# Narrowing the feed-forward weights in other groups: w_out shifted by one block, a transpose of q in two pieces

## The chip, the cores and the metric

The kernel runs on one core of one Trainium2 chip. A core has five engines that run side by side: TensorE (PE in the profile, with its weight loads as PEld), VectorE (DVE), ScalarE (ACT), GpSimd (POOL) and SyncE (SP), which here issues most of the transfers. The metric is the device time of one execution in microseconds (us), as the median of three runs: 303.51 us before the change (303.37 to 304.15).

## The reference

Two blocks follow one another. The first is a linear attention with a polynomial sketch: q and k are projected by S1 and S2, and the outer product of the two projections is the feature map. Its numerator divided by its denominator is the input x of a gated feed-forward layer.

```python
# batch, heads, seq, head_dim = 4, 4, 1088, 32;  r = 8
def phi(x):
    a = np.einsum('rd,bhsd->bhsr', S1, x)
    b = np.einsum('rd,bhsd->bhsr', S2, x)
    return np.einsum('bhsi,bhsj->bhsij', a, b).reshape(*x.shape[:-1], r * r)
q_p, k_p = (phi(q), phi(k))
kv = np.einsum('bhsf,bhsd->bhfd', k_p, v)
z = np.sum(k_p, axis=2)
num = np.einsum('bhsf,bhfd->bhsd', q_p, kv)
den = np.einsum('bhsf,bhf->bhs', q_p, z)[..., None] + 1e-06
attn = num / den                       # -> x: (4352 tokens, 128)

# w_gate, w_val: (128, 1536);  w_out: (1536, 128)
gate = 1.0 / (1.0 + np.exp(-(x @ w_gate)))
val = x @ w_val
out = gate * val @ w_out
```

S1, S2 and the three weights arrive as 64-bit floats, since they were divided by a 64-bit square root. The kernel sees each as two 32-bit words and has to narrow it to a 32-bit float itself, with integer operations.

## The kernel before

The 1536 hidden columns are 12 blocks (NJ = 12) of 128. The 4352 tokens are taken in chunks of 512 and a rest of 256. One "wave" (`w1`) multiplies a chunk by one block of w_gate and one of w_val; ScalarE takes the sigmoid; `glu` multiplies gate by val on VectorE; `w2` multiplies the product by the block of w_out and adds it to the chunk's output in PSUM. `slot` runs waves and puts the `w2` of a block behind the wave of the next.

```python
def slot(group, waves):
    if group is not None:
        group()
    todo = moe["todo"]
    for _ in range(waves):
        ...
        glu()                      # product of the wave before
        ...                        # lag = 2 (3 at the very end)
        while len(todo) >= lag:
            w2(*todo.pop(0))       # second layer, one block behind
        if more:
            w1()                   # next wave
```

The narrowing of one group of weights is a generator. Its steps use three engines; the caller decides between which other instructions each step is placed. PE, VectorE, ScalarE and GpSimd carry out their instructions in the order of the program.

```python
def narrow(out, bits, eng, bank=None, copies=None):
    cap, tail = tmp(I32, "cap", 6), tmp(I32, "tail", 5)
    eng.tensor_scalar(out=cap.bitcast(F32), in0=hi..., ...)        # GpSimd
    nc.scalar.activation(out=tail, in_=lo, func=ACTF.Copy, ...)    # ScalarE
    yield                                                          # step 0
    head = tmp(I32, "head", 3)
    nc.vector.tensor_scalar(out=head, in0=cap, ...)                # L105
    nc.vector.scalar_tensor_tensor(out=head, in0=cap, ..., in1=head, ...)  # L109
    yield                                                          # step 1
    square = cap.bitcast(F32)
    if bank:
        square = pso.tile([P, 512], F32, tag=bank, name="square")...
    nc.scalar.activation(out=square, in_=cap.bitcast(F32), func=ACTF.Square)
    nc.gpsimd.tensor_tensor(out=head, in0=head, in1=tail, op=ALU.add)      # L118
    yield                                                          # step 2
    nc.vector.scalar_tensor_tensor(out=out, in0=square, ..., in1=head, ...)  # L127
    yield                                                          # step 3
```

`pso` holds one tile per tag in PSUM, and its tags "acc0" and "acc1" are one bank each. The outputs of even chunks accumulate in acc0, those of odd ones in acc1; while one is in use the other is free for squares and for the denominators.

The groups before the change are: gate and val of block 0, gate and val of block 1, w_out of blocks 0 and 1 together (256 elements in a row each), then for j = 2 to 11 gate, val and w_out of block j (384 elements). A wave of chunk 0 carries the steps of the blocks that follow:

```python
def narrow_w(j, step):
    ...
        narrowing[j] = narrow(
            w_sb[:, :, j, :], w_in[n][:, :, jj], nc.gpsimd, "acc1" if j < NJ - 2 else None)

# in w1, after the sigmoid:
if ci == 0:
    if j0 == 1:
        narrow_01(2, 3)
    if 0 < j0 < NJ - 2:
        narrow_w(j0 + 1, 3)
    narrow_w(j0 + 2, 1)
    narrow_w(j0 + 2, 2)
    if j0 < 3:
        narrow_w(j0 + 3, 0)
    if j0 > 1:
        narrow_w(j0 + 4, 0)
```

Chunk 0 is interleaved with the rest of batch 0. Its second half of tokens needs a compact projection of q (`qcomp`, tile cqps), which goes out to DRAM and comes back spread over the partitions (`spread`, tiles qp and bq), a product of the two (`qmult`), and then denominators and numerators (`dn`, tiles dps and nps).

```python
def dn(b, n, mid=None, pool=(ps2, "two")):
    if b == 0:
        bank = (moe["sum"] + 1) % 2 if moe["sum"] >= 0 else 1
        dps = pso.tile([P, TCH], F32, tag=f"acc{bank}", name="dps")
    ...                                  # PE: dps, then nps
    def divide(...):
        ...                              # turn, add 1e-6, first(), reciprocal, transpose, product

slot(None, 1)                            # wave 0
slot(None, 1)                            # wave 1
turn_q(0, 1)                             # transpose of q, 576 wide, VectorE
slot(None, 1)                            # wave 2
slot(q01, 6)                             # cqps and spread, then waves 3 to 8
qmult(0, 1)
load_kq(1)
slot(None, 1)                            # wave 9
slot(lambda: part01(lambda: narrow_w(NJ - 1, 3)), 1)   # dn(0, 1), wave 10
slot(last01, 1)                          # last product of x, wave 11
```

Of the kernel before, what the change touches and what calls it, by code (L numbers as in the profile page):

```python
# [8 lines left out]
F32 = mybir.dt.float32  # L9
I32 = mybir.dt.int32  # L10
# [10 lines left out]
def kernel(  # L21
# [30 lines left out]
    const = ctx.enter_context(tc.tile_pool(name="const", bufs=1))  # L52
    ld = ctx.enter_context(tc.tile_pool(name="ld", bufs=1))
    sbA = ctx.enter_context(tc.tile_pool(name="sbA", bufs=2))
    raw = ctx.enter_context(tc.tile_pool(name="raw", bufs=NJ // 2))
    sbN = ctx.enter_context(tc.tile_pool(name="sbN", bufs=1))
    sbG = ctx.enter_context(tc.tile_pool(name="sbG", bufs=6))

# [24 lines left out]
    def narrow(out, bits, eng, bank=None, copies=None):  # L83

        p, n, m = bits.shape[:3]
        lo, hi = bits[:, :, :, 0].bitcast(U32), bits[:, :, :, 1]

        def tmp(dt, tag, bufs):
            return sbN.tile([P, 3, P], dt, tag=tag, name=tag, bufs=bufs)[:p, :n, :m]

        cap, tail = tmp(I32, "cap", 6), tmp(I32, "tail", 5)
        eng.tensor_scalar(  # L97
            out=cap.bitcast(F32), in0=hi.bitcast(F32), scalar1=122880.0, scalar2=-122880.0,
            op0=ALU.min, op1=ALU.max,
        )  # L100
        nc.scalar.activation(out=tail, in_=lo, func=ACTF.Copy, scale=2.0**-29)  # L101
        yield

        head = tmp(I32, "head", 3)
        nc.vector.tensor_scalar(  # L105
            out=head, in0=cap, scalar1=3, scalar2=0x3FFFFFF8,
            op0=ALU.logical_shift_left, op1=ALU.bitwise_and,
        )
        nc.vector.scalar_tensor_tensor(  # L109
            out=head, in0=cap, scalar=-0x40000000, in1=head, op0=ALU.bitwise_and, op1=ALU.bitwise_or  # L110
        )
        yield
        square = cap.bitcast(F32)
        if bank:
            square = pso.tile([P, 512], F32, tag=bank, name="square")[:, : n * m]
            square = square.rearrange("p (n m) -> p n m", n=n)
        nc.scalar.activation(out=square, in_=cap.bitcast(F32), func=ACTF.Square)  # L117
        nc.gpsimd.tensor_tensor(out=head, in0=head, in1=tail, op=ALU.add)  # L118
        yield

        head = head.bitcast(F32)
        if copies:
            square, head = (
                bass.AP(tensor=x.tensor, offset=x.offset, ap=[list(x.ap[0]), [0, copies], [1, m]])
                for x in (square, head)
            )
        nc.vector.scalar_tensor_tensor(  # L127
            out=out, in0=square, scalar=1.265625 * 2.0**-30, in1=head, op0=ALU.is_ge, op1=MUL
        )
        yield  # L130
# [11 lines left out]
                nc.sync.dma_start(out=rows, in_=s_)  # L142


    w_sb = const.tile([P, 3, NJ, P], F32, tag="w_sb", name="w_sb")
    w_in = {}

    def load_w_in(j0, j1):
        cs = slice(j0 * P, j1 * P)
        n, jj = divmod(j0, 2)  # L150
        if wide and jj == 0:
            w_in[n] = raw.tile([P, 3, 2, P, 2], I32, tag="w_in", name="w_in")
        for i, src in enumerate((moe_w_gate, moe_w_val)):
            if wide:
                nc.sync.dma_start(
                    out=w_in[n][:, i, jj : jj + j1 - j0].rearrange("p j m w -> p (j m w)"),
                    in_=src[:, cs].bitcast(I32),
                )
            else:
                nc.sync.dma_start(  # L160
                    out=w_sb[:, i, j0:j1].rearrange("p j m -> p (j m)"), in_=src[:, cs]
                )

    def load_w_out(n):
        j0, j1 = 2 * n, 2 * n + 2
        cs = slice(j0 * P, j1 * P)
        src = moe_w_out[cs, :].bitcast(I32) if wide else moe_w_out[cs, :]
        nc.sync.dma_start(
            out=w_in[n][:, 2].rearrange("p j m w -> p j (m w)") if wide else w_sb[:, 2, j0:j1],
            in_=src.rearrange("(j p) m -> p j m", p=P),  # L170
        )

    narrowing = {}

    def narrow_w(j, step):
        if not 0 <= j < NJ:
            return
        n, jj = divmod(j, 2)
        if wide:
            if step == 0:  # L180
                narrowing[j] = narrow(
                    w_sb[:, :, j, :], w_in[n][:, :, jj], nc.gpsimd, "acc1" if j < NJ - 2 else None
                )
            next(narrowing[j])


    def narrow_01(part, step):
        if wide:
            if step == 0:
                i = (slice(0, 2), part) if part < 2 else (2, slice(0, 2))  # L190
                narrowing["01", part] = narrow(
                    w_sb[:, i[0], i[1]],
                    w_in[0][:, i[0], i[1]],
                    nc.gpsimd,
                    "acc0" if part else "acc1",
                )
            next(narrowing["01", part])


    def load_rows(src, b, t, parts=((0, T, nc.sync),)):  # L200
# [42 lines left out]
    load_w_in(0, 1)  # L243
    v_t[0] = load_v(0)
    load_w_in(1, 2)
    load_w_out(0)
    load_rows(q, 0, q_t[0], ((T0, T, nc.sync),))
    for n in range(1, NJ // 2):
        load_w_in(2 * n, 2 * n + 2)
        load_w_out(n)  # L250


    def warm(*cols):
# [53 lines left out]
    def w2(ci, j0, jn, g):  # L307
# [4 lines left out]
        for jj in range(jn):  # L312
            j = j0 + jj
            nc.tensor.matmul(  # L314
                out=moe["acc"][:, :tw],
                lhsT=w_sb[:, 2, j, :],
                rhs=g[:, jj, :tw],
                start=(j == 0),
                stop=(j == NJ - 1),
            )  # L320
        if j0 + jn == NJ:
# [6 lines left out]
            while c < t0 + tw:  # L328
# [13 lines left out]
                    )  # L342
                c += n * 32

    def w1():

        ci = moe["ci"]
        t0, tw = tok_chk[ci]
        jn = TCH // tw
        j0 = moe["w"] * jn  # L350
        wv = psm.tile([P, 2, TCH], F32, tag="wave", name="wave")

        tp = tw // 2 if ci == 0 and j0 == 0 else tw
        for o in range(0, tw, tp):
            for which in range(2):
                for jj in range(jn):
                    nc.tensor.matmul(  # L357
                        out=wv[:, which, jj * tw + o : jj * tw + o + tp],
                        lhsT=w_sb[:, which, j0 + jj, :],
                        rhs=xT[:, t0 + o : t0 + o + tp],  # L360
                        start=True,
                        stop=True,
                    )
        sg = sbG.tile([P, TCH], F32, tag="sg", name="sg", bufs=3)
        nc.scalar.activation(out=sg, in_=wv[:, 0], func=ACTF.Sigmoid)  # L365
        if ci == 0:
            if j0 == 1:
                narrow_01(2, 3)
            if 0 < j0 < NJ - 2:
                narrow_w(j0 + 1, 3)  # L370
            narrow_w(j0 + 2, 1)
            narrow_w(j0 + 2, 2)
            if j0 < 3:
                narrow_w(j0 + 3, 0)
            if j0 > 1:
                narrow_w(j0 + 4, 0)


        def glu():
            g = sbG.tile([P, TCH], F32, tag="g", name="g")  # L380
            nc.vector.tensor_tensor(out=g, in0=wv[:, 1], in1=sg, op=MUL)  # L381
            moe["todo"].append((ci, j0, jn, g.rearrange("p (j t) -> p j t", j=jn)))

        moe["gate"] = glu
        moe["w"] += 1
        if j0 + jn == NJ:
            moe["ci"] += 1
            moe["w"] = 0
# [38 lines left out]
            in_=k_t[b][:, t0:t1].rearrange("p t d -> p (t d)"),  # L427
        )

    def turn_q(b, n):  # L430
        if b >= B:
            return
        if n == 0:
            qT_of[b] = sbA.tile([P, TP, 2, 32], F32, tag="qT", name="qT", bufs=1)
        t0, tn = q_chk[n]
        nc.vector.transpose(  # L436
            out=qT_of[b][:, t0 : t0 + tn].rearrange("p t c s -> p (t c s)"),
            in_=q_t[b][:, 2 * t0 : 2 * (t0 + tn)].rearrange("p t d -> p (t d)"),
# [214 lines left out]
    def qmult(b, n):  # L653
        q0 = half(QP[b], n)
        nc.vector.tensor_tensor(out=q0, in0=q0, in1=half(BQ[b], n), op=MUL)  # L655

    def kv0(j_list):
        if 0 not in KVZ:
# [34 lines left out]
            )  # L693

    def kvd(b):
        KVD[b] = sbA.tile([P, 2, 2, F], F32, tag="kvd", name="kvd")
        k0 = KVZ[b][:, : 2 * F]
        n = 2 if b > 0 else 1
        nc.scalar.copy(
# [211 lines left out]

    if wide:
        steps = narrow(s4, s_in, nc.vector, copies=4)
        for _ in range(3):
            next(steps)
    turn_k(0, 0, KBASE[2] + 1)
    if wide:
# [54 lines left out]
    for part in range(2):  # L972
        narrow_01(part, 0)
    spread_z()
    warm(512)
    for pi in range(2):
# [6 lines left out]
    def rest(turn, rc, dT):  # L983
# [8 lines left out]
        narrow_01(0, 1)  # L992
        narrow_01(0, 2)
        ndt(0)

    divide = dn(0, 0, rest)
    warm(256)

    def head1():
        narrow_01(1, 1)  # L1000
        narrow_01(0, 3)
        narrow_01(1, 2)
        narrow_01(2, 0)
        narrow_w(2, 0)

    divide((0, 4), (4, 8), between=head1)
    narrow_01(1, 3)
    narrow_01(2, 1)
    narrow_01(2, 2)

    slot(None, 1)
    cq = {}
# [33 lines left out]
        kv(b, ZS[b])  # L1046
        kvd(b)

    slot(None, 1)
    turn_q(0, 1)  # L1050
    slot(None, 1)
    slot(q01, 6)
    qmult(0, 1)
    load_kq(1)
    slot(None, 1)
    slot(lambda: part01(lambda: narrow_w(NJ - 1, 3)), 1)
    slot(last01, 1)
    v_t[1] = load_v(1)
    for b in range(1, B):
# [60 lines left out]
```

## Time and profile before

| | before |
|---|---|
| median of three runs | 303.51 us |
| span in the profile | 301.7 us |
| PE busy | 295.3 us (98%) |
| VectorE busy | 154.7 us (51%) |
| ScalarE busy | 80.7 us (27%) |
| GpSimd busy | 33.0 us (11%) |
| first wave starts | 15.18 us |
| last narrowing ends (L127) | 45.0 us |
| wave 0 of chunk 1 starts | 48.35 us |

The table is an average over stages. Up to 15 us the attention of the first tokens is computed; from 15 to 48 us chunk 0 runs beside the narrowing and the second part of batch 0, and VectorE is busy for 7.96 of 8.40 us between 15.18 and 23.58 and 13.56 of 17.39 between 23.58 and 40.97; afterwards the matmuls follow one another, and the attention of batches 1 to 3 lies between them. In the profile a matmul of 512 columns in 32-bit floats is two records, so a wave counts four.

### The profile page before, as it was taken

What the parts mean: (1) busy time and instruction counts of PE and PEld (TensorE: products, weight loads), DVE (VectorE), ACT (ScalarE), POOL (GpSimd) and SP (SyncE); (2) the same over time, 40 slices, a digit from 0 to 9 for tenths busy, and PEclk for the clock granted to TensorE, in tenths of its full rate; (3) what the DMA queues carried; (4) which work ended last, traced back from release to release, by engine and by line L of the source; (5) the groups of instructions that cost most, each with busy time, mean ns of one, the idle gap of its engine ahead of it and who ended that gap; (6) DMA issues with size and microseconds to landing.
All of it is one profiled execution on the core that took longest, in us unless ns stands there. A gap on an engine that the chain in (4) does not pass through costs nothing.

```text
span 301.7 us, 3642 instructions
## 1 busy us (share of the span) xinstructions
PE 295.3 (98%) x1363; PEld 137.3 (46%) x1363; DVE 154.7 (51%) x268; ACT 80.7 (27%) x150; POOL 33.0 (11%) x62
## 2 busy tenths in 40 slices
PE   8899999999999999999999999999999999999994
PEld 3444434453444444434444445344444444444683
DVE  6997789764635545383365444932232223222331
ACT  3556533222122222212232222122222222222220
POOL 1465550410000400000004000000000000000000
PEclk9999999999999999999999999999999999999999
DMA  7993440897101591350016900200020000100011
GB/s 226 358 337 89 103 144 6 201 223 192 42 15 19 136 225 35 77 187 0 0 27 168 218 17 2 36 2 0 0 32 3 0 0 12 25 0 0 9 28 18
DMA packets 30546, 24.24 MB, mean 80 GB/s; under 512 B 20480, under 2 KB 25728, under 8 KB 30528
## 3 DMA queue, kind: packets, MB, share of 16 engines
q1 hardware_dynamic: 27024, 16.15, 20.5%
q0 software_dynamic: 2592, 7.08, 10.5%
q10 hardware_dynamic: 912, 0.77, 1.0%
q8 instruction: 11, 0.18, 0.2%
q14 instruction: 7, 0.06, 0.1%
HBM read 20.73 MB, written 3.26 MB: 80 GB/s over the span
## 4 chain that ended last, share of the span: by engine, by line
PE 86%; DVE 5%; DMA 3%; issue 2%; POOL 2%; ACT 1%; SPq 0%; DVEq 0%; POOLq 0%; ACTq 0%
PE wave L357 52%; PE moeout L314 27%; DMA bq<-dq 2%; PE nps L861 2%; POOL head L118 1%; PE kvz L677 1%; DVE head L109 1%; DVE w_sb L127 1%; DVE qp L655 1%; DMA s_in<-in_S_dram 1%; PE kps L456 1%; DVE head L105 1%; PE cqps L602 0%; PE deni L811 0%; PE dps L841 0%
## 5 line engine op out<-in xcount | busy, mean ns | idle before, releaser
L357 PE MATMUL wave<-xT,w_sb 128*128 128x512 f32 (+1 forms) x436 | 191.6, 565 | 0.0
L381 DVE TENSOR_TENSOR g<-wave,sg 128x512 f32<-128x512 f32 x102 | 70.3, 689 | 131.0 <-ACT sg L365 130.7
L357 PEld LDWEIGHTS wave<-xT,w_sb 128*128 128x128 f32 x436 | 82.8, 190 | 93.0 <-issue 85.7
L365 ACT ACTIVATE sg<-wave 128x512 f32<-128x512 f32 x102 | 60.9, 597 | 197.8 <-PE wave L357 197.8
L314 PE MATMUL moeout<-g,w_sb 128*128 128x512 f32 (+1 forms) x216 | 105.2, 575 | 0.3 <-DVE w_sb L127 0.3
L314 PEld LDWEIGHTS moeout<-g,w_sb 128*128 128x128 f32 x216 | 39.9, 190 | 44.8 <-issue 38.9
L118 POOL TENSOR_TENSOR head<-head,tail 128x384 int32<-128x384 int32 (+2 forms) x14 | 13.4, 954 | 18.2 <-DVE head L109 14.0
L627 POOL DMA_DIRECT2D qp<-dq x6 | 3.5, 583 | 105.9 <-DMA dq<-cq 105.9
L535 DVE TENSOR_TENSOR kp<-kab 128x1152 f32<-128x1152 f32 (+2 forms) x10 | 10.5, 1070 | 0.0
L655 DVE TENSOR_TENSOR qp<-qp,bq 128x1152 f32<-128x1152 f32 (+1 forms) x7 | 9.0, 1288 | 0.0
L258 PE MATMUL warm<-const-float32-1.0 128*128 128x512 f32 (+1 forms) x12 | 7.1, 720 | 0.8 <-PEq L1104 0.8
L109 DVE SCALAR_TENSOR_TENSOR head<-cap,head 128x384 int32<-128x384 int32 (+2 forms) x14 | 7.5, 535 | 0.5
L127 DVE SCALAR_TENSOR_TENSOR w_sb<-square,head 128x384 f32<-128x384 f32 (+1 forms) x11 | 5.7, 518 | 3.9 <-POOL head L118 3.9
L324 DVE STREAM_TRANSPOSE o_sb<-moeout 128x512 f32<-128x512 f32 (+1 forms) x9 | 6.1, 678 | 1.4 <-PE moeout L314 1.3
L627 POOL DMA_DIRECT2D bq<-dq x12 | 6.7, 574 | 0.5 <-DVE g L381 0.2
L101 ACT ACTIVATE tail<-w_in 128x384 int32<-128x384 uint32 (+1 forms) x13 | 6.6, 521 | 0.2 <-DMA w_in<-in_moe_w_gate_dram 0.2
L97 POOL TENSOR_SCALAR cap<-w_in 128x384 f32<-128x384 f32 (+1 forms) x13 | 6.4, 502 | 0.0
L886 DVE TENSOR_TENSOR xT<-nps,rb 128x576 f32<-128x576 f32 (+2 forms) x9 | 5.9, 660 | 0.5
L861 PE MATMUL nps<-qp,nd 64*32 64x256 f32 (+1 forms) x128 | 5.5, 402 | 0.5 <-ACT nd L741 0.4
L436 DVE STREAM_TRANSPOSE qT<-kq 128x512 f32<-128x512 f32 (+1 forms) x8 | 5.7, 716 | 0.0
L117 ACT ACTIVATE square<-cap 128x384 f32<-128x384 f32 (+1 forms) x11 | 5.1, 463 | 1.8 <-DVE w_sb L127 1.7
L425 DVE STREAM_TRANSPOSE kT<-kq 128x1088 f32<-128x1088 f32 (+2 forms) x5 | 5.3, 1068 | 0.0
(89 smaller groups left out, 85.6 us busy)
## 6 DMA issues: line engine op xcount, KB each, us to landing
qp<-dq POOLq DMA_DIRECT2D x6, 576.0 KB, 7.5
bq<-dq POOLq DMA_DIRECT2D x12, 288.0 KB, 9.8
v<-in_v_dram SPq DMA_DIRECT2D x16, 144.0 KB, 4.5
kq<-in_k_dram SPq DMA_DIRECT2D x3, 544.0 KB, 3.9
kq<-in_q_dram SPq DMA_DIRECT2D x3, 544.0 KB, 4.8
w_in<-in_moe_w_out_dram SPq DMA_DIRECT2D x6, 256.0 KB, 7.2
w_in<-in_moe_w_gate_dram SPq DMA_DIRECT2D x5, 256.0 KB, 6.1
w_in<-in_moe_w_val_dram SPq DMA_DIRECT2D x5, 256.0 KB, 6.8
```

Of the source, the lines that this page charges most:

```text
L109: nc.vector.scalar_tensor_tensor(out=head, in0=cap, scalar=-0x40000000, in1=head, op0=ALU.bitwise_and, op1=ALU.bitwise_or)
L118: nc.gpsimd.tensor_tensor(out=head, in0=head, in1=tail, op=ALU.add)
L127: nc.vector.scalar_tensor_tensor(out=out, in0=square, scalar=1.265625 * 2.0**-30, in1=head, op0=ALU.is_ge, op1=MUL)
L258: nc.tensor.matmul(out=t[:, 0, :n], lhsT=x, rhs=r, start=True, stop=True)
L314: nc.tensor.matmul(out=moe["acc"][:, :tw], lhsT=w_sb[:, 2, j, :], rhs=g[:, jj, :tw], start=(j == 0), stop=(j == NJ - 1),)
L357: nc.tensor.matmul(out=wv[:, which, jj * tw + o : jj * tw + o + tp], lhsT=w_sb[:, which, j0 + jj, :], rhs=xT[:, t0 + o : t0 + o + tp], sta ...
L365: nc.scalar.activation(out=sg, in_=wv[:, 0], func=ACTF.Sigmoid)
L381: nc.vector.tensor_tensor(out=g, in0=wv[:, 1], in1=sg, op=MUL)
L535: eng.tensor_tensor(out=KP[b][:, pi, j0:j1].rearrange("p j m (i l) -> p (j m) i l", i=R), in0=bass.AP(tensor=a0.tensor, offset=a0.offset, ...
L627: get.dma_start(out=t[64 * c : 64 * c + 64 if i else P, n * H * W1 : (n + 1) * H * W1], in_=bass.AP(tensor=d0.tensor, offset=d0.offset, ap ...
L655: nc.vector.tensor_tensor(out=q0, in0=q0, in1=half(BQ[b], n), op=MUL)
L861: nc.tensor.matmul(out=t[32 * h : 32 * h + 32, c, :w], lhsT=ND[b][rows, 32 * h : 32 * h + 32], rhs=half(QP[b], n)[rows, 2 * (h % 2) + h // ...
```

## The change

The groups of the narrowing are cut anew, so that a w_out block is narrowed one wave later than gate and val of the same block, when it is first needed:

- gate and val of block 2 are narrowed without w_out 2 (256 elements), and w_out 0 and w_out 1 each alone (128); from j = 3 on a group is gate j, val j and w_out j - 1 (384), and w_out 11 comes last alone (128). The tile w_sb gets one empty row of 128 columns, so that such a group is a slice with one stride; the raw tiles w_in and the transfers that fill them are cut in the same way.
- the head step of the narrowing becomes two steps, one for each of its instructions.
- the order of the steps in the waves is written anew, with the first step 0 two waves ahead moved from wave 2 to wave 6.
- the transpose of q for the second half is cut into a piece of 5 of its 9 parts and a piece of 4, put into waves 2 and 3; cqps and the spread come after wave 3 instead of after wave 2.
- squares go to a PSUM bank for all blocks up to j = 10, where it was up to j = 9.
- kvd has one buffer in place of two.

The core of the diff (tile shapes and the loads are left out, also parameters that keep their default):

```diff
+        yield                 # between the two head instructions of narrow
...
+    def load_w_out(j0, j1):
...
+    def narrow_w(part, *steps):
+        for step in steps if part in places else ():
             if step == 0:
+                at, bits, bank = places[part]
+                narrowing[part] = narrow(w_sb[:, at], bits, nc.gpsimd, bank)
+            next(narrowing[part])
+
+    places = {}
+    for j in range(NJ if wide else 0):
+        bits = w_in[j // 2][:, :, j % 2]
+        if j < 3:
+            at = slice(j, j + NJ + 1, NJ)
+            places["gv", j] = at, bits[:, :2], f"acc{1 - j % 2}"
+        else:
+            at = slice(j, j + 2 * NJ + 1, NJ)
+            places[j] = at, bits, "acc1" if j < NJ - 1 else None
+    if wide:
+        for j, bank in enumerate(("acc0", None)):
+            places["out", j] = (
+                slice(2 * NJ + 1 + j, 2 * NJ + 2 + j), w_in[j][:, 2, 1 - j : 2 - j], bank
+            )
+        places[NJ] = slice(3 * NJ, 3 * NJ + 1), w_in[NJ // 2][:, 0], None
...
-    load_w_out(0)
+    load_w_out(0, 1)
+    load_w_out(1, 2)
     load_rows(q, 0, q_t[0], ((T0, T, nc.sync),))
     for n in range(1, NJ // 2):
         load_w_in(2 * n, 2 * n + 2)
-        load_w_out(n)
+        if n == 1:
+            load_w_out(2, 3)
+        else:
+            load_w_out(2 * n - 1, 2 * n + 1)
+    load_w_out(NJ - 1, NJ)
...
         if ci == 0:
-            ...                                # as shown above
+            if j0 == 0:
+                narrow_w(("gv", 2), 1, 2, 3)
+                narrow_w(("out", 0), 4)
+                narrow_w(3, 0)
+            elif j0 == 1:
+                narrow_w(("gv", 2), 4)
+                narrow_w(("out", 1), 1, 2, 3)
+                narrow_w(3, 1, 2)
+                narrow_w(("out", 1), 4)
+                narrow_w(3, 3)
+                narrow_w(4, 0)
+            else:
+                if j0 in between:
+                    between[j0]()
+                if j0 != NJ - 2:
+                    narrow_w(j0 + 1, 4)
+                narrow_w(j0 + 2, 1, 2, 3)
+                if j0 <= 6:
+                    narrow_w(j0 + 3, 0)
+                if j0 >= 6:
+                    narrow_w(j0 + 4, 0)
...
     def head1():
-        narrow_01(1, 1)
-        narrow_01(0, 3)
-        narrow_01(1, 2)
-        narrow_01(2, 0)
-        narrow_w(2, 0)
+        narrow_w(("gv", 1), 1, 2)
+        narrow_w(("gv", 0), 4)
+        narrow_w(("gv", 1), 3)
+        narrow_w(("out", 0), 0)
+        narrow_w(("gv", 2), 0)
+        narrow_w(("out", 1), 0)
 
     divide((0, 4), (4, 8), between=head1)
-    narrow_01(1, 3)
-    narrow_01(2, 1)
-    narrow_01(2, 2)
+    narrow_w(("gv", 1), 4)
+    narrow_w(("out", 0), 1, 2, 3)
...
-    slot(None, 1)
-    turn_q(0, 1)
-    slot(None, 1)
-    slot(q01, 6)
+    between.update({2: lambda: turn_q(0, 1, 0, 5), 3: lambda: turn_q(0, 1, 5)})
+    slot(None, 3)
+    slot(q01, 5)
     qmult(0, 1)
     load_kq(1)
     slot(None, 1)
-    slot(lambda: part01(lambda: narrow_w(NJ - 1, 3)), 1)
+    slot(lambda: part01(lambda: narrow_w(NJ - 1, 4)), 1)
```

More of the change, by code (lines that the diff above doesn't have):

```diff
@@ L54 @@
     sbA = ctx.enter_context(tc.tile_pool(name="sbA", bufs=2))
-    raw = ctx.enter_context(tc.tile_pool(name="raw", bufs=NJ // 2))
+    raw = ctx.enter_context(tc.tile_pool(name="raw", bufs=1))
     sbN = ctx.enter_context(tc.tile_pool(name="sbN", bufs=1))
@@ L142, in load_s @@
                 nc.sync.dma_start(out=rows, in_=s_)
-    w_sb = const.tile([P, 3, NJ, P], F32, tag="w_sb", name="w_sb")
-    w_in = {}
+    w_sb = const.tile([P, 3 * NJ + 1, P], F32, tag="w_sb", name="w_sb")
+    w_in = []
+    for n in range(NJ // 2 + 1 if wide else 0):
+        shape = [3, 2] if n < NJ // 2 else [1, 1]
+        w_in.append(raw.tile([P] + shape + [P, 2], I32, tag=f"w_in{n}", name="w_in"))
     def load_w_in(j0, j1):
@@ L150, in load_w_in @@
         n, jj = divmod(j0, 2)
-        if wide and jj == 0:
-            w_in[n] = raw.tile([P, 3, 2, P, 2], I32, tag="w_in", name="w_in")
         for i, src in enumerate((moe_w_gate, moe_w_val)):
@@ L160, in load_w_in @@
                 nc.sync.dma_start(
-                    out=w_sb[:, i, j0:j1].rearrange("p j m -> p (j m)"), in_=src[:, cs]
-                )
[L164 to L171, printed above, removed]
@@ L173 @@
-    narrowing = {}
[L175 to L179, printed above, removed]
-            if step == 0:
[L181 to L197, printed above, removed]
+                    out=w_sb[:, i * NJ + j0 : i * NJ + j1].rearrange("p j m -> p (j m)"),
@@ new lines, in load_w_in @@
+                    in_=src[:, cs],
+                )
+    def load_w_out(j0, j1):
+        src = moe_w_out[j0 * P : j1 * P, :]
+        to = w_sb[:, 2 * NJ + 1 + j0 : 2 * NJ + 1 + j1]
+        if wide:
+            n, jj = divmod(j0 + 1, 2)
+            to = w_in[n][:, 2 if n < NJ // 2 else 0, jj : jj + j1 - j0]
+            to = to.rearrange("p j m w -> p j (m w)")
+            src = src.bitcast(I32)
+        nc.sync.dma_start(out=to, in_=src.rearrange("(j p) m -> p j m", p=P))
+    narrowing = {}
@@ L200, in load_rows @@
+    if wide:
+        for j, bank in enumerate(("acc0", None)):
[3 more added lines that the diff above has]
+        places[NJ] = slice(3 * NJ, 3 * NJ + 1), w_in[NJ // 2][:, 0], None
     def load_rows(src, b, t, parts=((0, T, nc.sync),)):
@@ L315, in w2 @@
                 out=moe["acc"][:, :tw],
-                lhsT=w_sb[:, 2, j, :],
+                lhsT=w_sb[:, 2 * NJ + 1 + j, :],
                 rhs=g[:, jj, :tw],
@@ L343, in w2 @@
                 c += n * 32
+    between = {}
     def w1():
@@ L358, in w1 @@
                         out=wv[:, which, jj * tw + o : jj * tw + o + tp],
-                        lhsT=w_sb[:, which, j0 + jj, :],
+                        lhsT=w_sb[:, which * NJ + j0 + jj, :],
                         rhs=xT[:, t0 + o : t0 + o + tp],
@@ L366, in w1 @@
         if ci == 0:
[L367 to L376, printed above, removed]
+            if j0 == 0:
[19 more added lines that the diff above has]
+                    narrow_w(j0 + 4, 0)
         def glu():
@@ L428, in turn_k, with turn_q @@
         )
-    def turn_q(b, n):
+    def turn_q(b, n, u0=0, u1=None):
         if b >= B:
@@ L435, in turn_q @@
         t0, tn = q_chk[n]
+        t0, tn = t0 + u0, (u1 or tn) - u0
         nc.vector.transpose(
@@ L651, in spread, with qmult @@
                     )
-    def qmult(b, n):
-        q0 = half(QP[b], n)
-        nc.vector.tensor_tensor(out=q0, in0=q0, in1=half(BQ[b], n), op=MUL)
+    def qmult(b, n, h0=0, h1=H):
+        q0, b0 = half(QP[b], n)[:, h0:h1], half(BQ[b], n)[:, h0:h1]
+        nc.vector.tensor_tensor(out=q0, in0=q0, in1=b0, op=MUL)
     def kv0(j_list):
@@ L695, in kvd @@
     def kvd(b):
-        KVD[b] = sbA.tile([P, 2, 2, F], F32, tag="kvd", name="kvd")
+        KVD[b] = sbA.tile([P, 2, 2, F], F32, tag="kvd", name="kvd", bufs=1)
         k0 = KVZ[b][:, : 2 * F]
@@ L913 @@
         steps = narrow(s4, s_in, nc.vector, copies=4)
-        for _ in range(3):
+        for _ in range(4):
             next(steps)
@@ L971 @@
         outer(0, pi, NJK - 1, NJK, eng=nc.gpsimd)
-    for part in range(2):
-        narrow_01(part, 0)
+    narrow_w(("gv", 0), 0)
+    narrow_w(("gv", 1), 0)
     spread_z()
@@ L991, in rest @@
         kvd(0)
-        narrow_01(0, 1)
-        narrow_01(0, 2)
+        narrow_w(("gv", 0), 1, 2, 3)
         ndt(0)
```

## The prediction

> **What bounds the kernel now.** I read the chain that ended last first, because it says which engine the end hangs on.
>
> ```profile
> PE 86%; DVE 5%; DMA 3%; issue 2%; POOL 2%; ACT 1%; SPq 0%; DVEq 0%; POOLq 0%; ACTq 0%
> ```
>
> PE holds 86% of the chain. The merged PE timeline shows its beat from 23.58 us on: 1.72 us of first-layer matmuls (two of 512 columns, two records each) and 0.86 us of second-layer ones, a wave every 2.575 us. A changed instruction off PE matters only where PE waits for it. The change touches nothing before the first wave (15.18 us), where even the regrouped narrowing keeps its order for blocks 0 and 1, and little after the last narrowing (45.0 us). So I next read the PE timeline of that stretch, leaving the steady waves out:
>
> ```profile
> 15.18 3.71 PE L357 MATMUL wave<-xT,w_sb 128*128 128x256 f32 x12
> 19.23 1.12 PE L314 MATMUL moeout<-g,w_sb 128*128 128x512 f32 x2 [0.34 <-DVE w_sb L127]
> 20.19 1.88 PE L357 MATMUL wave<-xT,w_sb 128*128 128x512 f32 x4
> 22.00 0.69 PE L602 MATMUL cqps<-qT,skq 64*32 64x288 f32 x8
> 22.62 1.13 PE L314 MATMUL moeout<-g,w_sb 128*128 128x512 f32 x2
> 23.58 1.88 PE L357 MATMUL wave<-xT,w_sb 128*128 128x512 f32 x4
> ...
> 39.03 1.88 PE L357 MATMUL wave<-xT,w_sb 128*128 128x512 f32 x4
> 40.97 0.69 PE L841 MATMUL dps<-qp,zb 128*32 128x288 f32 x8
> 41.59 0.71 PE L861 MATMUL nps<-qp,nd 64*32 64x288 f32 x16
> 42.24 1.12 PE L314 MATMUL moeout<-g,w_sb 128*128 128x512 f32 x2
> 43.20 1.88 PE L357 MATMUL wave<-xT,w_sb 128*128 128x512 f32 x4
> ```
>
> Columns are start and duration in us. Without waits, wave 3 would start at 15.18 + 2 x 1.72 + 2.575 + 0.62 (cqps) + 0.96 = 22.8; it starts at 23.58. So at most 0.8 us can be won at the front: half a microsecond before 19.23, the rest in small waits. From there to 40.97 PE hardly waits.
>
> The list of waits between 15 and 52 us names the causes (total, times, longest):
>
> ```profile
> PEld wave L357 <- DVE w_sb L127: 2.4, 6, 0.5
> ...
> PEld moeout L314 <- DVE w_sb L127: 1.2, 1, 1.2
> ...
> PEld dps L841 <- DVE qp L655: 0.9, 1, 0.9
> ```
>
> Every PE wait there is for VectorE: for a narrowed weight or for the multiplied spread qp. Last I read VectorE's and GpSimd's timeline at the end of the narrowing, blocks 9 and 10:
>
> ```profile
> 38.23 0.56 DVE L127 SCALAR_TENSOR_TENSOR w_sb<-square,head 128x384 f32<-128x384 f32 x1 [0.60 <-POOL head L118]
> 38.70 0.35 DVE L105 TENSOR_SCALAR head<-cap 128x384 int32<-128x384 int32 x1
> 39.09 0.56 DVE L109 SCALAR_TENSOR_TENSOR head<-cap,head 128x384 int32<-128x384 int32 x1
> 39.56 1.35 DVE L655 TENSOR_TENSOR qp<-qp,bq 128x1152 f32<-128x1152 f32 x1
> 40.83 0.69 DVE L381 TENSOR_TENSOR g<-wave,sg 128x512 f32<-128x512 f32 x1
> 41.81 0.56 DVE L127 SCALAR_TENSOR_TENSOR w_sb<-cap,head 128x384 f32<-128x384 f32 x1 [0.30 <-POOL head L118]
> ```
>
> ```profile
> 39.82 1.96 POOL L118 TENSOR_TENSOR head<-head,tail 128x384 int32<-128x384 int32 x1 [1.12 <-DVE head L109]
> ```
>
> Two things are to be seen. The narrowing is a loop across two engines: last step of block j (0.56), first two of block j+1 (0.35, 0.56), the GpSimd add (1.00), again the last step. Its last steps end 2.62 us apart (33.54, 36.16, 38.79), a little over PE's 2.575. And block 10 reads its square from "cap", in SBUF, while block 9 read "square", in PSUM bank acc1. That matters below.
>
> **What the Trainium skill says.** "Trainium Architecture — The Big Picture", section "Inside one NeuronCore": each engine has its own instruction stream and meets the others only through semaphores. The trace agrees: ScalarE and VectorE idle often while PE keeps its beat. So I can replay each engine's queue in program order with measured durations. "SBUF — State Buffer", section "Who interferes with whom": a VectorE instruction with two SBUF inputs contends with a GpSimd instruction that reads SBUF. The trace agrees: the add of block 10 lies under qmult (1.35 us) and takes 1.96 us in place of 1.00. "PSUM — Partial Sum Buffer", section "Summary: rules for kernel authors": for reading PSUM while matmuls run, a different bank is to be used, and the semaphores guard by bank. In this code a bank is one tile with one buffer, so a matmul into acc1 has to wait until the last reader of the tile before it is done; in the kernel before, that reader is block 9, finished at 38.79, and the trace shows no such wait. "VectorE: DVE Perf Modes", section on the TRN2 errata: a fixed extra latency per instruction. The trace agrees: the second head step takes 426 ns at 256 and 558 at 384 elements, a slope of 132 per 128, hence an estimate of 0.29 us for 128 and some 0.16 fixed.
>
> **The change, part by part.** I extend the two measured sizes to 128 elements in the same way (estimates): first head step 0.19, second 0.29, last step 0.27, GpSimd add 0.46.
>
> *Narrowing cut anew.* Before, 15.85 to 19.44 held the last step of block 1, two steps for w_out 0 and 1 together (256), two for all of block 2 (384, one of them stretched to 1.01), gate product 0, and only then the last step for w_out 0 and 1, which PE awaits at 19.23. Afterwards VectorE runs, from 16.26: w_out 0 (0.19 + 0.29), gate and val 2 (0.30 + 0.44), last step of w_out 0 (0.28): about 17.8. The sigmoid ends at 17.81, so product 0 ends at 18.53. PE has finished wave 1 at 18.7; w2(0) starts there and not at 19.23: **0.5 us won**. Then the last step of gate and val 2 (to 18.95), w_out 1 (0.5), block 3 (0.37 + 0.58), last step of w_out 1 (0.28), product 1 (0.68): 21.36. PE reaches w2(1) at 21.3. That fits closely.
>
> *The transpose of q in two, cqps one wave later.* The first piece (320 columns, about 0.50 between the measured 0.44 for 256 and 0.77 for 576) stands ahead of the last step of block 3: 21.36 + 0.50 + 0.57 = 22.43, so wave 3 starts at 22.47. Block 4's head steps end at 23.38, product 2 at 24.06, the second piece (0.42) at 24.48. PE is through with wave 3 at 24.19 and must wait for it: cqps starts at 24.53. With 0.62 for cqps and 0.96 for w2(2) wave 4 starts at 26.11; before, at 26.15. So the 0.5 us is **given back by 26 us**. The spread leaves two or three microseconds later; its data landed at 34.60 before and would land near 37, still ahead of qmult.
>
> *The loop.* Last step 4 ended at 25.32 before; now it waits for the add begun after 23.38 (latency 0.17 + 1.00) and ends near 25.13. From there the period is as before, and the double cap that stretched one turn to 2.98 (blocks 5 and 6 before) moves to blocks 9 and 10. Block 9 ends near 38.6, not 38.79.
>
> *The bank of block 10.* The rule "acc1 if j < NJ - 2" becomes "j < NJ - 1", so block 10 now squares into acc1. The next user of acc1 is dps, the denominators of the second part, which PE issues just after wave 9. Block 10's last step stands in VectorE's queue behind qmult (1.35), product 8 (0.69) and an add stretched to 1.96; it ended at 42.37 before and with the loop 0.2 us earlier ends at 42.17. So dps starts at 42.2 in place of 40.97: **+1.2 us**. Before, the same last step was hidden, since only wave 10 (43.20) needed it and 2.2 us of dps, nps and w2(8) lay between. Those matmuls now stand behind the wait.
>
> *w_out 11 alone.* One more narrowing of 128: 0.19 + 0.29 + 0.27 = 0.75 us of VectorE, in a stretch (41.8 to 50.35) in which it never idled. In the replay turn_k ends at 50.0 and both turns of q at 52.0, against cqps of batch 1 due at 50.67 + 1.2 = 51.9: +0.1 us. The two further DMA issues (0.4 us each) fall where weights are loaded ahead; kvd with one buffer waits for readers long done: 0.
>
> Sum: 303.51 + 1.2 + 0.1 = 304.8; I take **304.7**, as the replay may be late by a little.
>
> **The rivals.** (1) *The bank costs nothing* and the front gain lasts: dps would start when qmult ends, with VectorE earlier by 0.2 to 0.8 us, and the time would be 302.8 to 303.3. For it: somebody chose that bank. Against it: program order puts the last step of block 10 ahead of dps, and qmult ahead of both. (2) *The loop is the bound*: what VectorE gains or loses up to block 4 is handed on at 2.62 us per block, and PE waits for w_sb in every wave. The slack was only 26.15 - 25.32 = 0.83 us at block 4 and 39.03 - 38.79 = 0.24 at block 9. Should the contention at 17 us that stretched a 384 step to 1.01 hit the new sequence, the loop starts 0.3 to 0.5 us later than I have it, and the time is 305.1 to 305.4. (3) *A late spread*: if it landed after 39.5, qmult, dps and all behind would move with it. It has about 2.5 us in hand, so I give this little.
>
> **Range and chances.** The term that decides is the end of block 10's last step, 42.2 with some 0.4 either way from contention, and whether PE waits for it (I give that four in five). This gives **303.2 to 305.5**. Two per cent are 6 us, more than all that the touched stretch can win or lose: faster 0.01, same 0.98, slower 0.01.
>
> **What would show it.** Right: w2(0) near 18.7, cqps after a short wait for qT near 24.5, wave 4 near 26.1, and dps near 42.2 waiting for the last step of block 10. Wrong: dps within 0.2 us of the end of wave 9, or wave 4 before 25.6 with the gain still there at 50 us; PE waiting in waves 5 to 9 would point to rival 2.

## The result, and the profile after

The changed kernel takes 305.08 us (304.82 to 305.24, four runs), the kernel before 303.49 us in the same comparison. The ratio is 1.0047, with a 95% interval of 1.003 to 1.0065: slower by 1.6 us, and far from 2%. The prediction was 304.7, in a range of 303.2 to 305.5.

The chain that ended last, from the page of the changed kernel, by engine:

```profile
PE 91%; DVE 2%; issue 2%; POOL 2%; ACT 1%; DMA 1%; SPq 0%; DVEq 0%; POOLq 0%
```

PE's share went up from 86% to 91%. That tells little of the loss: the chain took other branches in the first 40 us, and a chain of 303 us hides a wait of 1.6. The PE timeline, by start and duration, shows where it is:

```profile
15.44 3.71 PE L374 MATMUL wave<-xT,w_sb 128*128 128x256 f32 x12
18.99 1.02 PE L329 MATMUL moeout<-g,w_sb 128*128 128x512 f32 x2
...
22.59 1.98 PE L374 MATMUL wave<-xT,w_sb 128*128 128x512 f32 x4
24.50 0.69 PE L632 MATMUL cqps<-qT,skq 64*32 64x288 f32 x8
25.12 1.12 PE L329 MATMUL moeout<-g,w_sb 128*128 128x512 f32 x2
26.08 1.88 PE L374 MATMUL wave<-xT,w_sb 128*128 128x512 f32 x4
...
38.95 1.94 PE L374 MATMUL wave<-xT,w_sb 128*128 128x512 f32 x4
42.48 0.69 PE L871 MATMUL dps<-qp,zb 128*32 128x288 f32 x8 [1.59 <-DVE w_sb L128]
...
52.18 0.69 PE L632 MATMUL cqps<-qT,skq 64*32 64x288 f32 x16
```

The first w2 no longer waits for its weight (18.99, without a bracket). Wave 4 starts at 26.08 (26.15 before), wave 9 at 38.95 (39.03). Then PE idles 1.59 us before dps, and the bracket names the releaser: line 128, the last step of a narrowing. dps starts at 42.48 in place of 40.97, and all behind it is as late: cqps, the projection of q, of batch 1 at 52.18 in place of 50.67. The line of the kernel before:

```profile
50.67 0.69 PE L602 MATMUL cqps<-qT,skq 64*32 64x288 f32 x16
```

The list of waits between 15 and 53 us (total, times, longest) has it twice, for the weight load of the matmul and for the matmul itself:

```profile
PEld dps L871 <- DVE w_sb L128: 2.4, 1, 2.4
...
PE dps L871 <- DVE w_sb L128: 1.6, 1, 1.6
```

VectorE and GpSimd at that point:

```profile
39.63 1.35 DVE L685 TENSOR_TENSOR qp<-qp,bq 128x1152 f32<-128x1152 f32 x1
40.90 0.69 DVE L410 TENSOR_TENSOR g<-wave,sg 128x512 f32<-128x512 f32 x1
41.87 0.56 DVE L128 SCALAR_TENSOR_TENSOR w_sb<-square,head 128x384 f32<-128x384 f32 x1 [0.28 <-POOL head L119]
```

```profile
39.89 1.94 POOL L119 TENSOR_TENSOR head<-head,tail 128x384 int32<-128x384 int32 x1 [1.12 <-DVE head L110]
```

qp, the input that dps waits for in the kernel before, is ready at 40.98. The last step of block 10 ends at 42.43 and dps starts 0.05 us later. It now reads "square", the bank acc1, where the kernel before reads "cap". VectorE's times there are almost those of before (this step ended at 42.37): the step is no slower, but PE now waits for it.

### The profile page after: what moved, and what is told of

It is laid out like the page before. It is cut to its first block, busy times and chain, and to the rows that moved or that the text cites. A ratio compares the mean times of both kernels' runs of the same rounds, so it can differ in the third digit from the quotient of the medians.

```text
span 303.4 us, 3667 instructions
## 1 busy us (share of the span) xinstructions
PE 295.6 (97%) x1363; PEld 137.0 (45%) x1363; DVE 155.7 (51%) x275; ACT 81.0 (27%) x154; POOL 33.7 (11%) x66
## 4 chain that ended last, share of the span: by engine, by line
PE 91%; DVE 2%; issue 2%; POOL 2%; ACT 1%; DMA 1%; SPq 0%; DVEq 0%; POOLq 0%
PE wave L374 56%; PE moeout L329 29%; PE nps L891 2%; PE kvz L707 1%; POOL head L119 1%; DMA s_in<-in_S_dram 1%; PE cqps L632 1%; PE kps L486 1%; PE deni L841 0%; PE dps L871 0%; PE kvz L693 0%; DVE qp L685 0%; DVE w_sb L128 0%; DVE o_sb L339 0%; POOL cap L97 0%
## 5 line engine op out<-in xcount | busy, mean ns | idle before, releaser
L119 POOL TENSOR_TENSOR head<-head,tail 128x384 int32<-128x384 int32 (+3 forms) x16 | 13.7, 858 | 19.8 <-DVE head L110 11.8
L110 DVE SCALAR_TENSOR_TENSOR head<-cap,head 128x384 int32<-128x384 int32 (+3 forms) x16 | 7.8, 487 | 0.6
L128 DVE SCALAR_TENSOR_TENSOR w_sb<-square,head 128x384 f32<-128x384 f32 (+2 forms) x12 | 6.0, 500 | 3.6 <-POOL head L119 3.6
L101 ACT ACTIVATE tail<-w_in 128x384 int32<-128x384 uint32 (+2 forms) x15 | 6.7, 473 | 1.0 <-DMA w_in<-in_moe_w_out_dram 1.0
L97 POOL TENSOR_SCALAR cap<-w_in 128x384 f32<-128x384 f32 (+2 forms) x15 | 6.8, 463 | 0.0
L466 DVE STREAM_TRANSPOSE qT<-kq 128x512 f32<-128x512 f32 (+3 forms) x9 | 5.8, 654 | 0.0
L118 ACT ACTIVATE square<-cap 128x384 f32<-128x384 f32 (+2 forms) x12 | 5.4, 447 | 1.6 <-DVE w_sb L128 1.5
```

Source lines behind the costliest of these rows:

```text
L97: eng.tensor_scalar(out=cap.bitcast(F32), in0=hi.bitcast(F32), scalar1=122880.0, scalar2=-122880.0, op0=ALU.min, op1=ALU.max,)
L110: nc.vector.scalar_tensor_tensor(out=head, in0=cap, scalar=-0x40000000, in1=head, op0=ALU.bitwise_and, op1=ALU.bitwise_or)
```

## The experiments

The start of the first wave differs between profiles, also of kernels whose code is the same up to it (14.88 to 15.73 us in ten of the eleven profiles here). So the table counts each profile from its own first wave. "cqps 1" is cqps of batch 1. From there to the last matmul every profile takes the same 246.88 to 246.91 us, and behind the last matmul 4.18 to 4.19 us in the kernel before and its variant, 4.28 to 4.33 us in the changed kernel and its variants. So apart from 0.1 us at the end, of open cause, and from the start of the first wave, the column "cqps 1" holds what a version wins or loses. All variants of the changed kernel have block 10 in SBUF.

| kernel | wave 4 | dps | cqps 1 | median us |
|---|---|---|---|---|
| before | 10.97 | 25.79 | 35.49 | 303.49 |
| changed | 10.64 | 27.04 | 36.74 | 305.08 |
| block 10 in SBUF | 10.63 | 25.53 | 35.81 | 303.99 |
| before, block 10 in PSUM | 10.98 | 27.24 | 36.94 | 305.00 |
| heads first | 11.14 | 26.59 | 36.29 | 304.75 |
| q whole | 10.42 | 25.70 | 35.97 | 304.13 |
| without w_out 11 | 10.62 | 25.56 | 35.26 | 303.42 |
| caps ahead | 10.92 | 26.41 | 36.11 | 303.62 |
| qmult early | 11.17 | 26.87 | 36.57 | 304.75 |
| turn_k early | 11.18 | 26.97 | 36.67 | 304.71 |
| all together | 10.76 | 26.50 | 36.20 | 304.35 |

The kernel before had a median of 303.56 beside the first four experiments, 303.48 beside the next four and 303.60 beside the last.

**Block 10 back in SBUF.**

```diff
-            places[j] = at, bits, "acc1" if j < NJ - 1 else None
+            places[j] = at, bits, "acc1" if j < NJ - 2 else None
```

> The changed kernel (305.08 us) with one condition set back: block 10 squares into its own buffer in SBUF, as in the kernel before. Theory (bank): dps no longer waits for the last step of block 10 (42.43 us) but only for qmult, which ends at 40.98 in VectorE's queue; dps starts near 41.0 and the time falls by 1.4 us to 303.6. Rival (the narrowing loop or VectorE's queue as a whole is late, the bank only names the wait): dps moves by less than 0.5 us, 304.6 to 305.1.

Measured 303.99 us, 1.09 less than the changed kernel (ratio to before 1.0015, 1.0008 to 1.0021). dps moved from 27.04 to 25.53 after the first wave, the 1.5 us of the theory:

```profile
39.00 1.88 PE L374 MATMUL wave<-xT,w_sb 128*128 128x512 f32 x4
41.02 0.69 PE L871 MATMUL dps<-qp,zb 128*32 128x288 f32 x8
...
50.21 0.72 PE L486 MATMUL kps<-kT,sk 64*32 64x288 f32 x16
51.30 0.72 PE L632 MATMUL cqps<-qT,skq 64*32 64x288 f32 x16 [0.37 <-DVE qT L466]
```

But the time is 0.4 us above the expected 303.6, and the last line says where most of it is lost: PE waits for the transpose of q of batch 1. From dps to cqps 1 it takes 10.28 us here; in the kernel before and in the changed one 9.70.

**The bank alone, in the kernel before.**

```diff
-                w_sb[:, :, j, :], w_in[n][:, :, jj], nc.gpsimd, "acc1" if j < NJ - 2 else None
+                w_sb[:, :, j, :], w_in[n][:, :, jj], nc.gpsimd, "acc1" if j < NJ - 1 else None
```

> The kernel before (303.49 us) with the bank condition of the change and nothing else of it: block 10 squares into acc1. Theory (bank): dps waits for the last step of block 10, which ends at 42.37 us there; it starts near 42.4 in place of 40.97, and the time rises by 1.4 us to 304.9. Rival (the loss comes from the regrouping, the later spread or the additional narrowing): the time stays within 0.3 us of 303.5.

Measured 305.00 us (ratio 1.0047, 1.0035 to 1.006), 1.44 more than before, and the same wait:

```profile
42.70 0.69 PE L841 MATMUL dps<-qp,zb 128*32 128x288 f32 x8 [1.51 <-DVE w_sb L127]
```

One number in one condition makes the kernel before as slow as the changed one; its step of block 10 takes 0.56 us as before and now holds PE up. With the first experiment this settles the bank as the cause: it brings the loss where it is set alone, and most of the loss goes where it alone is taken back.

**Without the narrowing of w_out 11.** This kernel leaves out part of the computation: the row of w_out 11 is filled with zeros.

```diff
-        places[NJ] = slice(3 * NJ, 3 * NJ + 1), w_in[NJ // 2][:, 0], None
...
+                if j0 == 8:
+                    nc.gpsimd.memset(w_sb[:, 3 * NJ], 0.0)
```

> As the first one (block 10 in SBUF, 303.99 us, dps at 41.02, cqps of batch 1 at 51.30), but the narrowing of w_out 11 is left out: GpSimd fills that row of w_sb with zeros, so the share of block 11 in the output is missing and VectorE is spared 0.18 + 0.29 + 0.28 us. Theory (with the bank wait gone, VectorE's queue carries those 0.75 us to the transpose of q of batch 1, and cqps of batch 1 waits for it): cqps starts near 50.7, the time falls by 0.5 us to 303.5. Rival (the rest of the loss lies at the front or in chance): within 0.15 us of 304.0.

Measured 303.42 us beside 303.48 for the kernel before (ratio 1.0001, 0.9985 to 1.0016), 0.57 less than with it (0.49 when each is taken against the kernel before that ran beside it). cqps 1 follows kps at once, 9.70 after dps:

```profile
49.86 0.71 PE L487 MATMUL kps<-kT,sk 64*32 64x288 f32 x16
50.37 0.69 PE L633 MATMUL cqps<-qT,skq 64*32 64x288 f32 x16
```

So the additional narrowing costs 0.5 to 0.6 us on PE, but only once the bank wait is gone. In the changed kernel VectorE used PE's pause to catch up (it idles 0.84 us before product 10), and the two losses lie over each other.

**The transpose of q whole again** (with block 10 in SBUF).

```diff
-    between.update({2: lambda: turn_q(0, 1, 0, 5), 3: lambda: turn_q(0, 1, 5)})
-    slot(None, 3)
-    slot(q01, 5)
+    slot(None, 1)
+    turn_q(0, 1)
+    slot(None, 1)
+    slot(q01, 6)
```

> As the first one (block 10 in SBUF), with the transpose of q whole again between waves 1 and 2 and cqps and the spread after wave 2, as in the kernel before; the regrouped narrowing stays. Theory (the half microsecond won at the front was given back by cqps waiting for the second piece): wave 4 starts near 25.8 in place of 26.08, but dps still waits for qmult in VectorE's queue near 41.0, so the time is that of the first one, 303.6. Rival (front gains reach the end): 303.2 to 303.3.

Measured 304.13 us (ratio 1.0021, 1.0012 to 1.0029), so no gain. The profiled execution took 307.62 us and began its first wave late, at 18.55 us, so only differences from there are used: wave 4 after 10.42, 0.55 less than before and 0.21 less than with the cut transpose; but dps after 25.70, no earlier than the 25.53 of the first experiment. The front gain is real, and VectorE takes it back before dps: the last step of block 9 ends at 42.07 and wave 9 starts at 42.13, 2.86 us after wave 8 instead of 2.575. There the narrowing loop holds PE, rival 2 of the prediction on a small scale.

**Breaking the narrowing loop.** Three trials, all with block 10 in SBUF. First the head steps of a block ahead of the last step of the block before it:

```diff
+                if j0 > 2:
+                    narrow_w(j0 + 2, 1, 2)
                 if j0 != NJ - 2:
                     narrow_w(j0 + 1, 4)
-                narrow_w(j0 + 2, 1, 2, 3)
+                narrow_w(j0 + 2, *((3,) if j0 > 2 else (1, 2, 3)))
```

> As the first one (block 10 in SBUF), and from wave 3 on VectorE does the two head steps of block j + 2 ahead of the last step of block j + 1, so that the GpSimd add has a whole wave and the loop of 2.62 us is broken. Theory (behind the bank the VectorE queue sets when qmult ends): VectorE has 2.05 us of work in a wave of 2.575, follows PE, and ends qmult near 39.7 to 40.3; dps starts as wave 9 ends, near 40.6 to 40.7, and the time is 303.1 to 303.3. Rival (PE's own beat sets the time from wave 4 on): as the first one, 303.6. A risk: the last step of block 4 comes 0.9 us later, just when wave 4 needs it (26.1).

Measured 304.75 us (ratio 1.0035, 1.0022 to 1.0047): slower than theory and rival had it. The loop stayed at 2.66 us, with another link, and now PE follows it: most waves start 2.66 to 2.68 us apart. VectorE and GpSimd:

```profile
25.40 0.36 DVE L105 TENSOR_SCALAR head<-cap 128x384 int32<-128x384 int32 x1 [0.74 <-POOL cap L97]
25.79 0.56 DVE L110 SCALAR_TENSOR_TENSOR head<-cap,head 128x384 int32<-128x384 int32 x1
```

```profile
23.88 0.99 POOL L119 TENSOR_TENSOR head<-head,tail 128x384 int32<-128x384 int32 x1 [1.16 <-ACT tail L101]
24.84 0.52 POOL L97 TENSOR_SCALAR cap<-w_in 128x384 f32<-128x384 f32 x1
```

The first head step needs the cap, and the cap stood behind the add of the block before in GpSimd's queue. The risk named in the expectation came true as well: wave 4 waited for its weight. The second trial keeps the order and puts the caps two waves ahead:

```diff
-                if j0 <= 6:
-                    narrow_w(j0 + 3, 0)
-                if j0 >= 6:
-                    narrow_w(j0 + 4, 0)
+                narrow_w(j0 + 4, 0)
```

Caps 4 and 5 go into wave 1 (not shown).

> The heads-first order once more (it took 304.75 us, since the first head step then waited for the GpSimd cap, which stood behind the add), now with the caps two waves ahead, so that no step of block j + 3 waits for the add of block j + 2. Theory (two queues in lockstep made the loop of 2.66 us): VectorE follows the sigmoid with a period of 2.575, waves 5 to 9 don't wait for w_sb, and dps starts at the end of wave 9 or of qmult, 40.7 to 41.2 for a first wave at 15.45; the time is 303.6 to 304.0. Rival [...]: a period of 2.66 stays, and 304.5 or more.

Measured 303.62 us (ratio 1.0009, 0.9989 to 1.0028), not to be told from the kernel before. Now VectorE idles for the sigmoid and the loop is gone: the last steps from 30.75 us on end 2.49 to 2.62 us apart, and waves 5 to 9 follow at 2.575. So delays between VectorE and GpSimd don't keep a loop of 2.66 us whatever the order. VectorE in waves 8 and 9:

```profile
36.34 0.69 DVE L410 TENSOR_TENSOR g<-wave,sg 128x512 f32<-128x512 f32 x1 [0.60 <-ACT sg L382]
...
37.81 0.55 DVE L128 SCALAR_TENSOR_TENSOR w_sb<-square,head 128x384 f32<-128x384 f32 x1
39.99 1.36 DVE L685 TENSOR_TENSOR qp<-qp,bq 128x1152 f32<-128x1152 f32 x1 [1.63 <-DMA bq<-dq]
```

But qmult waits 1.63 us for the spread, whose last piece lands at 39.87: the later cqps shows, as soon as VectorE is early enough to see it. So dps came after 26.41, not the 25.25 to 25.75 that the expectation makes from a first wave at 15.45; the time is at the lower edge of what was expected, though not for the reason given. The profiled execution, at 304.16 us, was 0.54 slower than the median. The last piece of bq lands 8.0 to 9.2 us after the first issue, over all profiles, and 9.2 after it here, so in other executions the wait may have been shorter; no run shows it.

The third trial puts the whole transpose back between waves 1 and 2 and cqps behind wave 2, so that the spread lands early, and qmult behind wave 7; a variant also puts the transpose of k of batch 1 ahead of the product of wave 10.

```diff
-    between.update({2: lambda: turn_q(0, 1, 0, 5), 3: lambda: turn_q(0, 1, 5)})
-    slot(None, 3)
+    slot(None, 1)
+    turn_q(0, 1)
+    slot(None, 1)
     slot(q01, 5)
     qmult(0, 1)
     load_kq(1)
-    slot(None, 1)
+    slot(None, 2)
     slot(lambda: part01(lambda: narrow_w(NJ - 1, 4)), 1)
+    turn_k(1)                 # in the variant only
     slot(last01, 1)
```

> As the one with caps ahead, with the transpose of q whole and cqps after wave 2 (as in the kernel before), and with qmult one wave earlier, after wave 7, where VectorE has idle time if the loop is broken. Theory: dps starts at the end of wave 9, about 25.15 us after the first wave (before: 25.79), and the transposes for batch 1 are less late; the time is 303.1 to 303.4. Rival (the 0.75 us of w_out 11 and the queue behind dps set cqps of batch 1 in any case): 303.6 to 304.0, with PE waiting before cqps of batch 1.

> As the one with qmult early, with the transpose of k of batch 1 ahead of the product of wave 10, where VectorE waits for the sigmoid. Theory (cqps of batch 1 is then no longer held by VectorE): 302.9 to 303.2, faster than both kernels. Rival (the product of wave 10 and x for chunk 1 come too late behind the transpose of k, 1.3 us): 303.6 or more, with PE waiting before wave 0 of chunk 1.

Measured 304.75 (ratio 1.0049, 1.0036 to 1.0061) and 304.71 us (1.0042, 1.0029 to 1.0054). Neither theory held. In the first of the two, VectorE and GpSimd:

```profile
36.06 2.00 DVE L685 TENSOR_TENSOR qp<-qp,bq 128x1152 f32<-128x1152 f32 x1
37.99 0.68 DVE L410 TENSOR_TENSOR g<-wave,sg 128x512 f32<-128x512 f32 x1
...
39.44 0.55 DVE L128 SCALAR_TENSOR_TENSOR w_sb<-square,head 128x384 f32<-128x384 f32 x1
```

```profile
35.85 1.00 POOL L119 TENSOR_TENSOR head<-head,tail 128x384 int32<-128x384 int32 x1 [1.13 <-DVE head L110]
```

The spread was there, but qmult met an add of GpSimd that had begun at 35.85 and took 2.00 us instead of 1.35; the weight of wave 9 came at 39.99 and PE waited before that wave instead of before dps. (0.3 us were already lost by wave 5, with waits of 0.33 us before cqps and 0.24 before wave 4.) The variant lost about as much in another way: there qmult took 1.36 us, but waited for the spread.

```profile
36.60 1.36 DVE L685 TENSOR_TENSOR qp<-qp,bq 128x1152 f32<-128x1152 f32 x1 [0.66 <-DMA bq<-dq]
```

PE was then late enough that cqps 1 did not wait (9.70 after dps in both), so the variant tells nothing of the transpose of k.

**All together.** The last kernel was to give qmult a place where no add meets it, and w_out 11 the idle time of waves 4 to 6.

```diff
+                elif j0 == 8:
+                    narrow_w(j0 + 2, 1)
+                    narrow_w(j0 + 1, 4)
                     between[j0]()          # qmult(0, 1)
+                    narrow_w(j0 + 2, 2, 3)
...
+                if j0 == 5:
+                    narrow_w(NJ, 1, 2, 3)
+                if j0 == 6:
+                    narrow_w(NJ, 4)
...
+                if j0 == 4:
+                    narrow_w(NJ, 0)
```

> What the runs point to, in one kernel: block 10's square in SBUF; caps two waves ahead; heads first from wave 4 on; the transpose of q whole and cqps after wave 2, so that the spread lands before it is needed; qmult in wave 8 between the first and the second head step of block 10, so that the GpSimd add of block 10 comes after it and neither blocks the other; w_out 11 narrowed in waves 4 to 6, where VectorE idles. Theory (VectorE's queue between the loop and cqps of batch 1 is the limit, and is now relieved of the loop, of the contention and of 0.75 us): counted from the first wave, dps starts after 25.1 to 25.4 us (before: 25.79) and cqps of batch 1 after 34.8 to 35.2 (before: 35.49), and the time is 0.3 to 0.7 us below the kernel before, 302.8 to 303.2. Rival (a new wait of about the same size, as in the last two trials): 303.5 or more.

Measured 304.35 us (ratio 1.0027, 1.002 to 1.0034): the rival. qmult took its undisturbed 1.35 us, but steps elsewhere met GpSimd and PE waited for weights in waves 5, 7 and 8:

```profile
27.00 0.87 DVE L105 TENSOR_SCALAR head<-cap 128x384 int32<-128x384 int32 x1
27.91 0.77 DVE L110 SCALAR_TENSOR_TENSOR head<-cap,head 128x384 int32<-128x384 int32 x1
...
31.27 0.87 DVE L105 TENSOR_SCALAR head<-cap 128x128 int32<-128x128 int32 x1
```

```profile
31.06 1.00 POOL L119 TENSOR_TENSOR head<-head,tail 128x384 int32<-128x384 int32 x1
```

```profile
29.20 1.98 PE L374 MATMUL wave<-xT,w_sb 128*128 128x512 f32 x4 [0.29 <-DVE w_sb L128]
```

None of these orders beats the kernel before.

## Why the prediction was right

*The bank.* This was the term that decided. Predicted: dps at 42.2, waiting for the last step of block 10, +1.2 us. Measured: 42.48, with a wait of 1.59 us whose releaser is that step. Both experiments on the bank alone confirm the cause. Counted from the first wave, dps moved by 1.25 us.

*The start of the first wave.* The prediction held it fixed at 15.18. It was 15.44 in this profile. Over the profiles of kernels with the same head it scatters by 0.85 us, so nothing here makes it an effect of the change. Counted from it, the last step of block 10 ended after 26.99 us, in the replay as in the trace, and dps started after 27.04 (replay: 27.02). In total, cqps 1 is later by 1.25 us and the end behind the last matmul longer by 0.1, against a predicted 1.3; the other 0.2 of the measured 1.6 is within what the first wave scatters.

*The front.* Predicted: w2(0) near 18.7, cqps near 24.5 after a short wait, wave 4 at 26.1 with the gain given back. Measured: 18.99, 24.50, 26.08. That the last two agree is luck, as the first wave was late by 0.26 us. Counted from there w2(0) came after 3.55 us (replay: 3.5), but cqps after 9.06 (9.35) and wave 4 after 10.64 (10.93; before 10.97). So 0.3 us of the front gain was not given back at 26 us; PE kept it up to dps, where it only made the wait longer, 1.59 us in place of the 1.3 that the replay gives. One reason why the replay was too slow is that it adds whole durations, while in the trace an instruction of VectorE often starts a little before the one ahead of it ends: the first piece of the transpose at 21.50, the product before it ended at 21.57. Two head steps that lay beside GpSimd instructions went the other way, 0.67 and 0.74 us where the replay had 0.44 and 0.58. With the whole transpose 0.55 us was kept at wave 4, so the cut cost 0.2.

*The loop.* Predicted: the period as before. Up to the double cap the last steps ended 2.66 to 2.68 us apart, before 2.62. In the changed kernel:

```profile
27.82 0.36 DVE L105 TENSOR_SCALAR head<-cap 128x384 int32<-128x384 int32 x1
```

```profile
27.25 0.54 POOL L97 TENSOR_SCALAR cap<-w_in 128x384 f32<-128x384 f32 x1
```

The head step starts as the cap of its own block ends. In the kernel before the caps are a wave further ahead from wave 2 on, here only from wave 6 on; there, too, the turn up to its double cap took 2.67 us. Counted from the first wave VectorE was 0.19 us ahead of the replay at block 4, and the longer turns took just that back by block 9; that the end of block 10 agreed to 0.01 us is luck too. Rival 2, that PE would wait for w_sb in each wave, did not come about in the changed kernel, but was close: its waves 4 to 9 follow at 2.575 us, and block 9's last step ended 0.09 us ahead of wave 9. The double cap moved as foreseen: the head step at 35.81 took 0.69 us.

*The spread.* The prediction had it landing at 34.60 before, near 37 after, with some 2.5 us in hand. But 34.60 is the landing of the first of the two transfers of bq. In the traces the last piece of the second landed at 37.13 before and at 38.08 in the changed kernel, 1.55 us ahead of qmult. No wait shows there; the trial with caps ahead, where it landed at 39.87, did wait. The rival was closer than I made it.

*w_out 11.* Predicted +0.1 us at cqps 1; in the changed kernel it was 0 (dps to cqps 1 took 9.70 us as before), behind a larger wait. Without the bank wait it is 0.5 to 0.6. The prediction rested on VectorE never idling in that stretch, which holds for the kernel before; behind the bank wait it idled 0.84 us, and that hid the additional work.

## What to carry to other kernels

With one tile per bank, as here, a scratch tile in a PSUM bank that matmuls also use ties the next matmul in that bank to the scratch's last reader. Before lending a bank, look in the program order for who takes it next and where its last reader stands in its own queue; here one more block of squares cost 1.4 to 1.5 us of PE time before dps, although the step that PE waits for took 0.56 us as before. And when a wait is removed, look for the next queue right behind it: the 0.5 to 0.6 us of w_out 11 could not be seen until the bank was free.

## What the runs showed of the hardware

Some instructions of VectorE and GpSimd delay each other in both directions, by which comes first: the GpSimd add took 1.94 us in place of 1.00 when it began under qmult, and qmult took 2.00 us in place of 1.35 when it came behind the start of an add. The small instructions suffer most in proportion: a head step over 128 elements took 0.18 us alone (in the changed kernel) and 0.87 behind an add (in the last one, shown above).

```profile
45.97 0.18 DVE L105 TENSOR_SCALAR head<-cap 128x128 int32<-128x128 int32 x1
```

Not every pair does this: in the changed kernel the product g, which reads the wave from PSUM, took 0.68 us from 31.36 on while an add began at 31.61 and took 1.00. I had counted on the delay for qmult but not for every head step that a new order moves; it is one reason why the reorderings, on paper worth up to 0.7 us, brought nothing.
